# Spreading operand preparation over half rounds, freeing a conversion buffer earlier, and respacing normalisation steps in a fused attention and expert kernel

## The chip, the cores and the metric

The kernel runs on one core of a Trainium2 chip. The metric is the device time of one execution in microseconds (us): the kernel before takes 2182.73 us, the median of three runs (2181.15 to 2185.93).

A core has five engines with a queue each, and each works its queue strictly in order: TensorE (PE: matrix products, with its weight loads listed apart as PEld), VectorE (DVE), ScalarE (ACT), GpSimd (POOL) and SyncE (SP), which here issues the DMA transfers. An instruction that waits holds everything behind it on its engine. Matrix products land in PSUM banks; all else lies in SBUF.

## The reference

```python
# attention: q, k, v of 4 x 8 heads x 576 x 64, causal by blocks of 64
x = attention(q, k, v)                      # 2304 tokens x 512
h = x @ w_in                                # 512 -> 2048
x = np.maximum(0.01 * h, h) @ w_out         # 2048 -> 512
P = exp(x @ w_gate - max)                   # 2304 x 8 experts
for _ in range(8):                          # the normalisation
    P /= P.sum(1) + 1e-9; P /= P.sum(0) + 1e-9; P *= 2304 / 8
out = sum over e of P[:, e:e+1] * (np.maximum(x @ w1[e], 0) @ w2[e])   # 512 -> 1024 -> 512
```

The first three parts feed one another. w_in and w_out arrive as 64-bit numbers; all else is float32.

## The kernel before

**Split operands.** TensorE multiplies a 32-bit format (fp32r) with fewer mantissa bits than float32. So each operand is split into a high part (a cast on ACT) and a low part (value minus high part, a subtraction on DVE), and a product is three: high by high, high by low, low by high. `w_split` does this for weights, `x_step` for x, `halves` for sums of weights. Tile names end in h and l accordingly (w1h, w1l, xhS, xlS).

**Stages.** After attention (to about 260 us) comes the first MLP: its 2048 hidden columns are taken in two halves (e = 0, 1), each in 8 chunks (f) of 128, and the tokens in five blocks of 512, 512, 512, 384 and 384. For each (e, block, f) `hidden` makes 128 hidden columns (L514) and `second` multiplies them by w_out into four PSUM banks o0 to o3 (L543), two chunks behind. At f = 7 the four banks are emptied into xa, for e = 0 by copies on ACT and DVE (L552, L554); the next block's first `second` needs those banks.

**Conversion.** The 64-bit weights are rebuilt from their words by `bits_steps`: six operations on DVE (begin L156, bound L160, shift L166, sign L172, power L178, rest L184), then for the second half of the weights an addition on POOL (`store`, L208) and a DMA to a scratch tensor in DRAM (s_in, s_out), from which half e = 1 loads its weights. Raw words lie in two buffers (wraw), intermediate words in two of wa and one of wb: wb is taken at shift and given back when POOL has read it. The list `bits` holds loads and steps of 16 such units; the main loop takes six entries from it after each chunk, from block 1 on (L857 to L860).

**The experts.** The second MLP runs in three passes of 768 tokens (p). Each pass has 8 experts of 4 column groups, taken two at a time: a round is 14 products of six matmuls (`product`, L733, the "half round") and then six combinations of twelve (`combine`, L787), 16 rounds in a pass, 48 in all. The products use fast-matrix-multiplication terms of x: A11, A12, A22 and sums S1 to S4, made by `x_step` (a subtraction on POOL, L717, in place in xa; the cast on ACT, L719; the low part on DVE, L720). A pass's last round must make the next pass's seven operands: this is called the turn here; there are two (pass 0 to 1 near 1170 us, 1 to 2 near 1672 us). In the turn `behind(...)` puts two operands behind each of the first three combinations and one behind the fourth, together with the round's usual work: the next groups' weights (`w1_sums` on POOL L679 to L682, `w1_s`, `w1_a` on ACT and DVE L695, L696, `w2_split` L131, L132) and the emptying of the output banks (L795 to L800).

**The normalisation** runs beside the first rounds: `gate_chunk` for six late token tiles, `gate_max`, `gate_exp`, then eight times `rows`, a small matmul for the column sums (L636) and `columns`; sums stand at fixed products and combinations.

**Order.** A scheduler puts each engine's queue in order from the order of the code and its own time estimates; `in_order` chains PE's products, and `behind` places steps after the latest relu instructions (`last_taken`).

Of the kernel before, what the change touches and what calls it, by code (L numbers as in the profile page):

```python
# [8 lines left out]
F32 = mybir.dt.float32  # L9
# [3 lines left out]
ALU = mybir.AluOpType  # L13
AX = mybir.AxisListType
# [22 lines left out]
def block_attention_mlp_moe(  # L37
# [15 lines left out]
    nc = tc.nc  # L53
# [92 lines left out]
    def bits_steps(which, f):  # L146
# [35 lines left out]
        def rest():  # L182
            bf = st["bf"] = st["b"].bitcast(F32)
            nc.vector.scalar_tensor_tensor(  # L184
                out=bf, in0=st["low"], scalar=2.0 ** -52, in1=bf, op0=ALU.mult, op1=ALU.mult
            )
# [316 lines left out]
    hid, o_ps = {}, {}  # L503
# [30 lines left out]
    def second(e, b, f):  # L534
# [3 lines left out]
        for s in range(KC):  # L538
# [7 lines left out]
            if f == FC - 1:  # L546
                at = t0
                while at < t0 + n:
                    p, to = at // TP, min(t0 + n, (at // TP + 1) * TP)
                    a, o = xv[p][:, s, at - p * TP:to - p * TP], o_ps[s][:, at - t0:to - t0]  # L550
                    if e == 0 and (p > t0 // TP if t0 // TP < (t0 + n - 1) // TP else s % 2):
                        nc.vector.tensor_copy(out=a, in_=o)  # L552
# [71 lines left out]
    def rows():  # L624
# [7 lines left out]
        nc.vector.tensor_reduce(out=st["cs"], in_=pr.rearrange("p t e -> p e t"), axis=AX.X, op=ALU.add)  # L632
# [78 lines left out]
    def x_step(p, k):  # L711
# [4 lines left out]
        if change:  # L716
            nc.gpsimd.tensor_tensor(out=src, in0=change[0], in1=change[1], op=ALU.subtract)  # L717
# [109 lines left out]
    for m, (e, b, f) in enumerate(todo):  # L827
# [23 lines left out]
        if e == 0 and b == 0:  # L851
            if f < len(late):
                bits_load(*late[f])
            if 0 < f <= len(late):
                for step in bits_steps(*late[f - 1]):
                    step()
        elif e == 0 and bits:  # L857
            for _ in range(6):
                if bits:
                    bits.pop(0)()  # L860
# [42 lines left out]
    norm = [gate_max, gate_exp, rows]  # L903
# [11 lines left out]
    order = [*range(TC // 2, TC), *range(TC // 2)]  # L915
    for n in range(0, NGR, 2):
        p, e, i = groups[n]
        turn = e == E - 1 and i + 2 == NI and p + 1 < NPASS
        for m, (g, k, name, begins, f, *a) in enumerate(first_products):
            product(n + g, k, name, begins)  # L920
            f(n + g, *a)
            if n == 0 and m in (1, 3, 5):
                in_order(gate_chunk)(NPASS - 1, TC // 2 + m // 2, o_bank())
            if n == 0 and m == 2:
                w2_split(1)
                w2_load(2)
                w2_load(3)
            if n and norm and m in (1, 4):
                normal(o_bank)
            if m == 5:  # L930
                w1_sums(n + 2)
                if not n:
                    norm.pop(0)()
        if owed and not norm:
# [6 lines left out]
            lambda: w2_split(n + 3),  # L941
            lambda: (w2_load(n + 4), w2_load(n + 5)),
        ]
        for m, t in enumerate(order):
            combine(n, t)
            if turn:
                behind(*(lambda k=k: x_step(p + 1, k) for k in terms[2 * m:2 * m + 2]))
            behind(more[m])
            if norm and m in ((0, 2, 5) if n == 0 else (2, 5)):
                normal(h_bank)  # L950
# [33 lines left out]
```

## Time and profile before

| | before |
|---|---|
| device time, median of 3 (lowest to highest) | 2182.73 us (2181.15 to 2185.93) |
| the profiled execution's own time | 2183.18 us |
| its span, first to last instruction | 2181.4 us |
| mean granted TensorE clock | 0.995 |
| busy PE / DVE / ACT / POOL | 2141.8 / 1473.5 / 917.2 / 510.2 us |

Busy shares say which engine is nearly always at work: PE, 98% of the span. Whatever shortens this kernel must therefore take work from PE or one of the stretches in which PE waits. The list of waits names these by the line that waited and the line that released it; "idle before" in a row of the timeline is the same wait at its place. Times in a timeline run from the span's start; a duration of one matmul is longer than the distance to the next, since matmuls overlap, so losses are read from start to start.

### The profile page before, as it was taken

What the parts mean: (1) busy time and instruction counts of PE and PEld (TensorE: products, weight loads), DVE (VectorE), ACT (ScalarE), POOL (GpSimd) and SP (SyncE); (2) the same over time, 40 slices, a digit from 0 to 9 for tenths busy, and PEclk for the clock granted to TensorE, in tenths of its full rate; (3) what the DMA queues carried; (4) which work ended last, traced back from release to release, by engine and by line L of the source; (5) the groups of instructions that cost most, each with busy time, mean ns of one, the idle gap of its engine ahead of it and who ended that gap; (6) DMA issues with size and microseconds to landing.
All of it is one profiled execution on the core that took longest, in us unless ns stands there. A gap on an engine that the chain in (4) does not pass through costs nothing.

```text
span 2181.4 us, 29500 instructions
## 1 busy us (share of the span) xinstructions
PE 2141.8 (98%) x10932; PEld 1904.3 (87%) x10932; DVE 1473.5 (68%) x2467; ACT 917.2 (42%) x1916; POOL 510.2 (23%) x549
## 2 busy tenths in 40 slices
PE   7999999999999999999999999999999999999999
PEld 6787787998899899899988989998898899989998
DVE  7999777343356866766677677666767766676665
ACT  6776522232334434443344344434443443344332
POOL 3334332000022122221223222222223221222220
PEclk9999999999999999999999999999999999999999
DMA  4333134020002122211222222122213212221120
GB/s 103 84 88 85 41 112 144 25 68 1 1 21 77 39 78 78 78 50 67 78 78 68 78 78 67 50 78 78 73 44 106 78 49 68 78 78 56 61 78 29
DMA packets 157248, 146.63 MB, mean 67 GB/s; under 512 B 62640, under 2 KB 126128, under 8 KB 157104
## 3 DMA queue, kind: packets, MB, share of 16 engines
q1 hardware_dynamic: 157104, 144.75, 22.1%
q8 instruction: 86, 1.41, 0.3%
q14 instruction: 58, 0.48, 0.1%
HBM read 135.81 MB, written 8.91 MB: 66 GB/s over the span
## 4 chain that ended last, share of the span: by engine, by line
PE 79%; DVE 3%; issue 0%; ACT 0%; POOL 0%; ACTq 0%; DVEq 0%
PE o L787 34%; PE h_ps L733 32%; PE o L543 7%; PE h_ps L514 6%; DVE w1l L696 1%; DVE xlS L720 0%; DVE w2l L132 0%; DVE xa L800 0%; PE l_ps L597 0%; DVE xa L795 0%; DVE xlA L720 0%; DVE c L750 0%; ACT w1h L695 0%; POOL xa L717 0%; PE o L586 0%
## 5 line engine op out<-in xcount | busy, mean ns | idle before, releaser
L787 PE MATMUL o<-w2h,xhlate 128*128 128x512 f32 x1152 | 402.4, 390 | 0.0
L787 PE MATMUL o<-w2h,xllate 128*128 128x512 f32 x1152 | 401.6, 389 | 0.0
L679 POOL TENSOR_TENSOR wa<-wraw 128x256 f32<-128x256 f32 x96 | 87.6, 912 | 1271.3 <-DVE w1l L696 1174.9
L741 ACT COPY s<-h_ps 128x384 f32<-128x384 f32 x288 | 138.5, 481 | 565.1 <-PE h_ps L733 565.1
L750 DVE TENSOR_TENSOR c<-h_ps,s 128x384 f32<-128x384 f32 x288 | 155.7, 555 | 324.8 <-PE h_ps L733 314.8
L733 PE MATMUL h_ps<-xhS,w1h 128*128 128x384 f32 x768 | 258.1, 336 | 0.0
L733 PE MATMUL h_ps<-xlS,w1h 128*128 128x384 f32 x768 | 257.4, 335 | 0.0
L733 PE MATMUL h_ps<-xhS,w1l 128*128 128x384 f32 x768 | 257.2, 335 | 0.0
L787 PEld LDWEIGHTS o<-w2h,xllate 128*128 128x128 f32 x1152 | 216.3, 188 | 45.4
L787 PEld LDWEIGHTS o<-w2h,xhlate 128*128 128x128 f32 x1152 | 216.2, 188 | 43.4
L800 DVE SCALAR_TENSOR_TENSOR xa<-o,pr,xa 128x512 f32<-128x512 f32 x264 | 189.6, 741 | 52.5 <-PE o L787 52.4
L787 PE MATMUL o<-w2l,xhlate 128*128 128x512 f32 x576 | 224.7, 390 | 0.0
L787 PE MATMUL o<-w2l,xllate 128*128 128x512 f32 x576 | 224.4, 390 | 0.0
L733 PE MATMUL h_ps<-xhA,w1l 128*128 128x384 f32 x576 | 194.1, 337 | 10.3 <-DVE w1l L696 10.3
L733 PE MATMUL h_ps<-xhA,w1h 128*128 128x384 f32 x576 | 193.6, 336 | 0.0
L733 PE MATMUL h_ps<-xlA,w1h 128*128 128x384 f32 x576 | 193.2, 335 | 0.0
L696 DVE TENSOR_TENSOR w1l<-wraw,w1h 128x512 fp32r<-128x512 f32 x192 | 175.8, 954 | 0.1
L696 DVE TENSOR_TENSOR w1l<-wa,w1h 128x512 fp32r<-128x512 f32 x192 | 166.8, 871 | 0.0
L756 ACT ACTIVATE xllate<-c 128x384 fp32r<-128x384 f32 x144 | 75.7, 525 | 185.0 <-DVE c L750 185.0
L132 DVE TENSOR_TENSOR w2l<-wraw,w2h 128x1024 fp32r<-128x1024 f32 x100 | 147.2, 1473 | 1.1 <-ACT w2h L131 1.1
L733 PEld LDWEIGHTS h_ps<-xhS,w1h 128*128 128x128 f32 x768 | 145.0, 189 | 0.0
L733 PEld LDWEIGHTS h_ps<-xlS,w1h 128*128 128x128 f32 x768 | 144.9, 189 | 0.0
(164 smaller groups left out, 4321.8 us busy)
## 6 DMA issues: line engine op xcount, KB each, us to landing
wraw<-in_moe_w_dram SPq DMA_DIRECT2D x192, 512.0 KB, 4.2
wraw<-in_moe_w_in_dram SPq DMA_DIRECT2D x16, 512.0 KB, 3.8
wraw<-in_moe_w_out_dram SPq DMA_DIRECT2D x16, 512.0 KB, 3.6
out_dram<-xa SPq DMA_DIRECT2D x18, 256.0 KB, 2.3
qraw<-in_q_dram SPq DMA_DIRECT2D x32, 128.0 KB, 2.4
kraw<-in_k_dram SPq DMA_DIRECT2D x32, 128.0 KB, 2.6
vz<-in_v_dram SPq DMA_DIRECT2D x32, 128.0 KB, 2.3
s_in<-wa SPq DMA_DIRECT2D x8, 256.0 KB, 3.1
```

The lines of the kernel that those rows point to most:

```text
L132: nc.vector.tensor_tensor(out=lo, in0=raw, in1=f32(hi), op=ALU.subtract)
L514: nc.tensor.matmul(ps[:, 0:n], w[:, c, cols], x, start=c == 0 and s == 0, stop=c == KC - 1 and s == 2,)
L543: nc.tensor.matmul(o_ps[s][:, 0:n], w[:, cut], h[:, 0:n], start=f == 0 and m == 0, stop=f == FC - 1 and m == 2)
L679: nc.gpsimd.tensor_tensor(out=one[:, 0], in0=a21, in1=a22, op=ALU.add)
L696: nc.vector.tensor_tensor(out=lo, in0=x, in1=f32(hi), op=ALU.subtract)
L733: mm = nc.tensor.matmul(ps, w[:, c], x[:, c], start=first and c == 0 and s == 0, stop=c == 1 and s == 2, skip_group_check=True,)
L741: nc.scalar.copy(out=t, in_=bank[n, name][:, 0:HT])
L750: nc.vector.tensor_tensor(out=c, in0=x, in1=part[n, add], op=ALU.add)
L756: nc.scalar.activation(out=hi, in_=x, func=AF.Relu),
L787: mm = nc.tensor.matmul(o, h, w, start=m == 0, stop=m == 11)
L800: nc.vector.scalar_tensor_tensor(out=a, in0=o, scalar=pr[:, tt, e:e + 1], in1=a, op0=ALU.mult, op1=ALU.add)
```

## The change

Four edits: the conversion's last DVE step writes into the raw buffer instead of wb for units of the second half; the conversion steps of e = 0 are taken only after chunks 1 to 6 of a block and stand behind the latest DVE copy of a block end; the normalisation's sums stand at other products and combinations; and the next pass's operands are made in three places (A11 and the subtractions of S1 and S3 at product 2 of the turn's round; S1, S2, S3 in its combinations; S4, A12, A22 from product 3 of the round after), with the subtractions on DVE rather than POOL for the passes after the first. One w2 split and one w2 load of the turn move to product 2 of the round after. The number of rounds, products and matmuls is the same.

```diff
         def rest():
-            bf = st["bf"] = st["b"].bitcast(F32)
+            bf = st["bf"] = (st["b"] if f < FC else st["low"]).bitcast(F32)
             nc.vector.scalar_tensor_tensor(
-                out=bf, in0=st["low"], scalar=2.0 ** -52, in1=bf, op0=ALU.mult, op1=ALU.mult
+                out=bf, in0=st["low"], scalar=2.0 ** -52, in1=st["b"].bitcast(F32), op0=ALU.mult, op1=ALU.mult
             )
...
-                        nc.vector.tensor_copy(out=a, in_=o)
+                        taken[:] = [nc.vector.tensor_copy(out=a, in_=o)]
...
-        nc.vector.tensor_reduce(out=st["cs"], in_=pr.rearrange("p t e -> p e t"), axis=AX.X, op=ALU.add)
+        t = nc.vector.tensor_reduce(out=st["cs"], in_=pr.rearrange("p t e -> p e t"), axis=AX.X, op=ALU.add)
+        last_taken.append(getattr(t, "ins", t))
...
-    def x_step(p, k):
+    def x_src(p, k, make):
...
-        if change:
-            nc.gpsimd.tensor_tensor(out=src, in0=change[0], in1=change[1], op=ALU.subtract)
+        if make and change:
+            eng = nc.vector if p else nc.gpsimd
+            eng.tensor_tensor(out=src, in0=change[0], in1=change[1], op=ALU.subtract)
+        return src
+
+    def x_step(p, k, make=True):
+        src = x_src(p, k, make)
...
-        elif e == 0 and bits:
-            for _ in range(6):
-                if bits:
-                    bits.pop(0)()
+        elif e == 0 and 0 < f < FC - 1:
+            with tc.issue_after(getattr(taken[0], "ins", taken[0])):
+                for _ in range(6):
+                    if bits:
+                        bits.pop(0)()
...
-            if n == 0 and m in (1, 3, 5):
-                in_order(gate_chunk)(NPASS - 1, TC // 2 + m // 2, o_bank())
-            if n == 0 and m == 2:
-                w2_split(1)
-                w2_load(2)
-                w2_load(3)
-            if n and norm and m in (1, 4):
+            if n == 0 and 0 < m <= TC // 2:
+                in_order(gate_chunk)(NPASS - 1, TC // 2 + m - 1, o_bank())
+            if (n == 0 or turned) and m == 2:
+                w2_split(n + 1)
+                if n == 0:
+                    w2_load(2)
+                w2_load(n + 3)
+            if turned and 2 < m < 6:
+                x_step(p, terms[m + 1])
+            if n == 0 and m == TC // 2:
+                gate_max()
+            if norm and m in ((1, 5) if n else (5,)):
                 normal(o_bank)
+            if turn and m == 2:
+                x_step(p + 1, "A11")
+                for k in ("S1", "S3"):
+                    x_src(p + 1, k, True)
...
-            lambda: w2_split(n + 3),
-            lambda: (w2_load(n + 4), w2_load(n + 5)),
+            lambda: None if turn else w2_split(n + 3),
+            lambda: (w2_load(n + 4), None if turn else w2_load(n + 5)),
         ]
         for m, t in enumerate(order):
             combine(n, t)
-            if turn:
-                behind(*(lambda k=k: x_step(p + 1, k) for k in terms[2 * m:2 * m + 2]))
+            if norm and m in (1, 4):
+                normal(h_bank)
             behind(more[m])
-            if norm and m in ((0, 2, 5) if n == 0 else (2, 5)):
-                normal(h_bank)
+            if turn and m < 3:
+                behind(lambda: x_step(p + 1, terms[m + 1], m == 1))
+        turned = turn
```

Line numbers of the changed kernel are one to six higher: L697 there is L696 here, L719 the subtraction, L725 and L726 the cast and low part of `x_step`, L806 is L800.

**Place 1: the end of block 1 of e = 0, DVE.** Before, in DVE's queue (wa, wb and wraw are the conversion's buffers, g and hl the hidden chunk, o0 to o3 the banks that are emptied):

```order
L160 TENSOR_SCALAR wa_4055<-wa_4055 128x512
L166 TENSOR_SCALAR wb_4058<-wa_4055 128x512
L522 TENSOR_TENSOR g_3694<-h_ps_3679,g_3694 128x512
L172 SCALAR_TENSOR_TENSOR wa_4055<-wraw_3973,wb_4058 128x512
L552 COPY xa1_2981<-o0_3407 128x256
L552 COPY xa1_2981<-o1_3411 128x256
L178 TENSOR_SCALAR wb_4058<-wa_4055 128x512
L156 TENSOR_SCALAR wa_4103<-wraw_4017 128x512
L524 TENSOR_TENSOR hl_3693<-g_3694,hh_3692 128x512
L552 COPY xa1_2981<-o2_3415 128x256
L184 SCALAR_TENSOR_TENSOR wb_4058<-wraw_3973,wb_4058 128x512
L552 COPY xa1_2981<-o3_3419 128x256
```

In the changed kernel at the same block end:

```order
L522 TENSOR_TENSOR g_3644<-h_ps_3629,g_3644 128x512
L524 TENSOR_TENSOR hl_3643<-g_3644,hh_3642 128x512
L522 TENSOR_TENSOR g_3685<-h_ps_3670,g_3685 128x512
L552 COPY xa1_2981<-o0_3407 128x256
L552 COPY xa1_2981<-o1_3411 128x256
L524 TENSOR_TENSOR hl_3684<-g_3685,hh_3683 128x512
L552 COPY xa1_2981<-o2_3415 128x256
L552 COPY xa1_2981<-o3_3419 128x256
L166 TENSOR_SCALAR wb_3778<-wa_3667 128x512
L156 TENSOR_SCALAR wa_3819<-wraw_3665 128x512
L172 SCALAR_TENSOR_TENSOR wa_3667<-wraw_3621,wb_3778 128x512
L160 TENSOR_SCALAR wa_3819<-wa_3819 128x512
```

Before, six conversion steps stand among these rows, ahead of the four copies and between them; now the copies stand behind hidden chunks alone, and the conversion goes on after the last. L184 now writes wraw.

**Place 2: the first turn, DVE and ACT.** Before, DVE's queue after the first output bank of the turn's combinations (xl is a low part of x, w1l and w2l those of weights, xa0 the output of the pass that ends, xa1 the x of the next):

```order
L720 TENSOR_TENSOR xlA11_10440<-xa1_2981,xhA11_10439 128x768
L696 TENSOR_TENSOR w1l_10449<-wa_10340,w1h_10448 128x512
L696 TENSOR_TENSOR w1l_10449<-wa_10341,w1h_10448 128x512
L696 TENSOR_TENSOR w1l_10455<-wraw_10204,w1h_10454 128x512
L696 TENSOR_TENSOR w1l_10455<-wraw_10204,w1h_10454 128x256
L800 SCALAR_TENSOR_TENSOR xa0_2980<-o2_10460,pr_2987,xa0_2980 128x512
L720 TENSOR_TENSOR xlS4_10509<-xa1_2981,xhS4_10508 128x768
L720 TENSOR_TENSOR xlA12_10513<-xa1_2981,xhA12_10512 128x768
L132 TENSOR_TENSOR w2l_10551<-wraw_10284,w2h_10550 128x1024
L800 SCALAR_TENSOR_TENSOR xa0_2980<-o3_10493,pr_2987,xa0_2980 128x512
L132 TENSOR_TENSOR w2l_10570<-wraw_10286,w2h_10569 128x1024
L720 TENSOR_TENSOR xlS1_10445<-xa1_2981,xhS1_10444 128x768
```

In the changed kernel, from the first output bank on:

```order
L697 TENSOR_TENSOR w1l_10446<-wa_10346,w1h_10445 128x512
L697 TENSOR_TENSOR w1l_10446<-wa_10347,w1h_10445 128x512
L697 TENSOR_TENSOR w1l_10452<-wraw_10204,w1h_10451 128x512
L806 SCALAR_TENSOR_TENSOR xa0_2980<-o2_10461,pr_2987,xa0_2980 128x512
L697 TENSOR_TENSOR w1l_10452<-wraw_10204,w1h_10451 128x256
L726 TENSOR_TENSOR xlS1_10458<-xa1_2981,xhS1_10457 128x768
L726 TENSOR_TENSOR xlS3_10517<-xa1_2981,xhS3_10516 128x768
L806 SCALAR_TENSOR_TENSOR xa0_2980<-o3_10489,pr_2987,xa0_2980 128x512
L132 TENSOR_TENSOR w2l_10538<-wraw_10284,w2h_10537 128x1024
L719 TENSOR_TENSOR xa1_2981<-xa1_2981 128x2x384
L697 TENSOR_TENSOR w1l_10505<-wa_10476,w1h_10504 128x512
```

The low parts of S4 and A12 have moved ahead of these rows (between the last relu steps of the round), that of A11 into the round's products, and one of two w2 splits too; S1 and S3 have moved from behind the w2 splits to ahead of the remaining one. The two casts that end this stretch on ACT, and what follows them, before:

```order
L695 CAST w1h_10516<-wa_10486 128x512
L719 CAST xhS2_10476<-xa1_2981 128x768
L719 CAST xhA22_10544<-xa1_2981 128x768
L741 COPY s1_10599<-h_ps_10592 128x384
L741 COPY s1_10608<-h_ps_10601 128x384
L741 COPY s5_10617<-h_ps_10610 128x384
```

and in the changed kernel:

```order
L696 CAST w1h_10504<-wa_10477 128x512
L725 CAST xhS2_10485<-xa1_2981 128x768
L725 CAST xhA22_10640<-xa1_2981 128x768
L747 COPY s1_10580<-h_ps_10573 128x384
L747 COPY s1_10589<-h_ps_10582 128x384
L747 COPY s5_10598<-h_ps_10591 128x384
```

They stand in the same places: the next round's first copies out of PSUM (s1, L741, now L747) remain behind the casts of S2 and A22.

**Place 3: the end of e = 0, DVE.** Before, ending with the first low part of e = 1's first chunk, hl_4613 (the w1l and w2l are weights of e = 1, loaded from the scratch tensors):

```order
L132 TENSOR_TENSOR w1l_4632<-wraw_4595,w1h_4631 128x1024
L522 TENSOR_TENSOR g_4502<-h_ps_4487,g_4502 128x384
L132 TENSOR_TENSOR w2l_4560<-wraw_4521,w2h_4559 128x1024
L524 TENSOR_TENSOR hl_4501<-g_4502,hh_4500 128x384
L522 TENSOR_TENSOR g_4538<-h_ps_4523,g_4538 128x384
L524 TENSOR_TENSOR hl_4537<-g_4538,hh_4536 128x384
L132 TENSOR_TENSOR w1l_4716<-wraw_4675,w1h_4715 128x1024
L522 TENSOR_TENSOR g_4578<-h_ps_4563,g_4578 128x384
L132 TENSOR_TENSOR w2l_4636<-wraw_4597,w2h_4635 128x1024
L524 TENSOR_TENSOR hl_4577<-g_4578,hh_4576 128x384
L522 TENSOR_TENSOR g_4614<-h_ps_4599,g_4614 128x512
L524 TENSOR_TENSOR hl_4613<-g_4614,hh_4612 128x512
```

In the changed kernel, up to the row before the same low part:

```order
L178 TENSOR_SCALAR wb_4516<-wa_4513 128x512
L184 SCALAR_TENSOR_TENSOR wraw_4425<-wraw_4425,wb_4516 128x512
L132 TENSOR_TENSOR w1l_4553<-wraw_4507,w1h_4552 128x1024
L522 TENSOR_TENSOR g_4535<-h_ps_4520,g_4535 128x384
L524 TENSOR_TENSOR hl_4534<-g_4535,hh_4533 128x384
L132 TENSOR_TENSOR w2l_4557<-wraw_4509,w2h_4556 128x1024
L522 TENSOR_TENSOR g_4578<-h_ps_4563,g_4578 128x384
L132 TENSOR_TENSOR w1l_4632<-wraw_4595,w1h_4631 128x1024
L524 TENSOR_TENSOR hl_4577<-g_4578,hh_4576 128x384
L132 TENSOR_TENSOR w2l_4636<-wraw_4597,w2h_4635 128x1024
L522 TENSOR_TENSOR g_4614<-h_ps_4599,g_4614 128x512
L132 TENSOR_TENSOR w1l_4716<-wraw_4675,w1h_4715 128x1024
```

The last conversion step (wraw_4425), which stood two blocks ahead, now stands among these chunks. The four weights between w1l_4553 and w1l_4716 follow it closely, and w1l_4716, two chunks ahead of hl_4613 before, stands directly in front of it.

## Rows read from the trace of the kernel before

**Rows 1.** Windows: length, busy PE, PEld, DVE, ACT, POOL with instructions, PE clock, DMA.

```profile
357.50:364.30 6.80, 5.85 (x14) 4.60 (x15) 6.50 (x13) 2.38 (x5) 1.28 (x1) 0.50 0.43 146
1176.70:1183.50 6.80, 3.78 (x12) 3.78 (x13) 6.80 (x8) 2.64 (x5) 5.68 (x6) 0.50 0.43 150
1200.00:1640.00 440.00, 440.00 (x2215) 399.00 (x2214) 300.33 (x428) 179.66 (x341) 103.08 (x116) 1.00 0.23 70
```

**Rows 2.** Waits of PE: what waited, releaser: us in all, times, longest.

```profile
PE h_ps L733 <- DVE w1l L696: 10.3, 2, 5.2
...
PE o L543 <- DVE xa L552: 4.3, 2, 3.1
...
PE h_ps L636 <- DVE cs L632: 0.8, 1, 0.8
...
PE o L636 <- ACT s L741: 0.6, 1, 0.6
PE o L636 <- DVE cs L632: 0.5, 1, 0.5
```

**Rows 3.** Chain that ended last, two rounds: start, us, what.

```profile
1194.91 16.36 PE o L787 x72
1211.27 14.58 PE h_ps L733 x84
```

**Rows 4.** Timeline, PE, end of block 1: start us, us, instruction, idle before it.

```profile
354.93 0.39 PE L514 MATMUL h_ps<-xhfirst,w1l 128*128 128x512 f32 x1
358.45 0.79 PE L543 MATMUL o<-hh,w2h 128*128 128x512 f32 x1 [3.13 <-DVE xa L552]
...
364.47 0.39 PE L543 MATMUL o<-hh,w2l 128*128 128x512 f32 x1
```

**Rows 5.** Timeline, PE, first turn.

```profile
1174.23 0.34 PE L733 MATMUL h_ps<-xlA,w1h 128*128 128x384 f32 x1
1179.72 0.69 PE L733 MATMUL h_ps<-xhA,w1l 128*128 128x384 f32 x1 [5.15 <-DVE w1l L696]
...
1183.64 0.34 PE L733 MATMUL h_ps<-xhS,w1l 128*128 128x384 f32 x1
```

**Rows 6.** Timeline, DVE, end of block 1.

```profile
356.43 0.43 DVE L166 TENSOR_SCALAR wb<-wa 128x512 uint32<-128x512 uint32 x1 [1.15 <-POOL wa L208]
...
357.38 0.68 DVE L172 SCALAR_TENSOR_TENSOR wa<-wraw,wb 128x512 uint32<-128x512 uint32 x1
357.98 0.75 DVE L552 COPY xa<-o 128x256 f32<-128x256 f32 x2
```

**Rows 7.** Timeline, DVE, combinations of an undisturbed round.

```profile
1196.99 0.56 DVE L757 SCALAR_TENSOR_TENSOR xllate<-c,xllate 128x384 fp32r<-128x384 f32 x1 [0.65 <-ACT xllate L756]
...
1201.57 1.76 DVE L132 TENSOR_TENSOR w2l<-wraw,w2h 128x1024 fp32r<-128x1024 f32 x1
...
1203.91 1.21 DVE L132 TENSOR_TENSOR w2l<-wraw,w2h 128x1024 fp32r<-128x1024 f32 x1
...
1205.64 1.56 DVE L696 TENSOR_TENSOR w1l<-wraw,w1h 128x512 fp32r<-128x512 f32 x2
1207.12 1.22 DVE L696 TENSOR_TENSOR w1l<-wa,w1h 128x512 fp32r<-128x512 f32 x1
```

**Rows 8.** Timeline, DVE, first turn.

```profile
1160.26 0.95 DVE L720 TENSOR_TENSOR xlA<-xa,xhA 128x768 fp32r<-128x768 f32 x1
...
1166.68 1.93 DVE L720 TENSOR_TENSOR xlS<-xa,xhS 128x768 fp32r<-128x768 f32 x1
```

**Rows 9.** Timeline, DVE, products of a round before the first turn.

```profile
1149.62 0.56 DVE L750 TENSOR_TENSOR c<-h_ps,s 128x384 f32<-128x384 f32 x1 [6.62 <-PE h_ps L733]
```

**Rows 10.** Timeline, ACT, first turn.

```profile
1179.15 0.83 ACT L719 CAST xhA<-xa 128x768 fp32r<-128x768 f32 x1 [1.38 <-POOL xa L717]
1179.89 0.47 ACT L741 COPY s<-h_ps 128x384 f32<-128x384 f32 x1
```

**Rows 11.** Timeline, POOL, first turn.

```profile
1165.77 2.02 POOL L717 TENSOR_TENSOR xa<-xa 128x768 f32<-128x768 f32 x1
1167.75 1.46 POOL L680 TENSOR_TENSOR wa<-wa,wraw 128x256 f32<-128x256 f32 x1
```

**Rows 12.** DMA issues: count, KB each, median us to landing.

```profile
wraw<-s_in SPq DMA_DIRECT2D x4, 512.0 KB, 4.3
```

**Rows 13.** Groups by line: count, busy us, mean ns, idle before.

```profile
L208 POOL TENSOR_TENSOR wa<-wa,wb 128x512 f32<-128x512 f32 x16 | 21.4, 1336 | 69.9 <-DVE wb L184 66.5 <-issue 3.5
```

**Rows 14.** Timeline, ACT, combinations of an undisturbed round.

```profile
1198.72 2.00 ACT L131 CAST w2h<-wraw 128x1024 fp32r<-128x1024 f32 x2
```

More of the change, by code (lines that the diff above doesn't have):

```diff
@@ L501, in block_attention_mlp_moe @@
     nc.gpsimd.tensor_tensor(out=gparts[:, :, 1, :], in0=gate, in1=f32(gparts[:, :, 0, :]), op=ALU.subtract)
-    hid, o_ps = {}, {}
+    hid, o_ps, taken = {}, {}, []
     def hidden(e, b, f):
@@ L901, in block_attention_mlp_moe @@
     ]
-    norm = [gate_max, gate_exp, rows]
+    norm = [gate_exp, rows]
     for n in range(SINKHORN):
@@ L915, in block_attention_mlp_moe @@
     order = [*range(TC // 2, TC), *range(TC // 2)]
+    turned = False
     for n in range(0, NGR, 2):
@@ L921, in block_attention_mlp_moe @@
             f(n + g, *a)
-            if n == 0 and m in (1, 3, 5):
-                in_order(gate_chunk)(NPASS - 1, TC // 2 + m // 2, o_bank())
-            if n == 0 and m == 2:
-                w2_split(1)
-                w2_load(2)
-                w2_load(3)
-            if n and norm and m in (1, 4):
+            if n == 0 and 0 < m <= TC // 2:
[10 more added lines that the diff above has]
+            if norm and m in ((1, 5) if n else (5,)):
                 normal(o_bank)
+            if turn and m == 2:
+                x_step(p + 1, "A11")
+                for k in ("S1", "S3"):
+                    x_src(p + 1, k, True)
             if m == 5:
                 w1_sums(n + 2)
-                if not n:
-                    norm.pop(0)()
         if owed and not norm:
```

## The prediction

> **What bounds the kernel now.** I read four views in this order. The windows first: over 440 us of the experts' rounds PE is busy for 440.00 us at clock 1.00 while DVE works 300 and POOL 103 [rows 1]. The reader should see that nothing but PE counts there, and that the change, which leaves every matmul in place, can gain nothing in such a stretch. Then the list of PE's waits: behind the start, the large ones at lines that the change touches are the two of 10.3 us together on w1l (the two turns), two of 4.3 us on the copies that empty the output banks (block ends, the longer 3.1 us), and three of the normalisation, 0.8 + 0.6 + 0.5 = 1.9 us [rows 2]. Third, the windows again: after the long waits PE runs at a granted clock of 0.50, which is 1.2 GHz instead of 2.4 GHz, in 357.5 to 364.3 and in 1176.7 to 1183.5 [rows 1]. So a wait costs more than its idle time, and a loss must be read from start to start. Last the chain, for the undisturbed distances: 72 matmuls of a combination phase take 16.36 us, 0.227 us each, and 84 of a product phase 14.58 us, 0.174 us each [rows 3].
>
> With these the losses are:
> - End of block 1: from the last matmul before the wait at 354.93 to the first at full pace at 364.47 there are 15 intervals [rows 4]. They took 9.54 us and are worth 15 x 0.227 = 3.41: loss 6.1.
> - The other block end: 4.3 - 3.1 = 1.2 us of wait [rows 2]; I take 1.2.
> - First turn: 13 intervals from 1174.23 to 1183.64 [rows 5] took 9.41 and are worth 2.26: loss 7.15. The second turn waits as long (10.3 is twice 5.2), so I take the same: 14.3.
> - Normalisation: 1.9.
>
> Together 23.5 us of 2183.18.
>
> **Block ends.** The cause shows in DVE's queue: at 356.43 a shift step (L166) has waited 1.15 us for POOL to give wb back, then come the hidden chunk, a sign step of 0.68 and only at 357.98 the copies that PE wants [rows 6]. In the changed order the conversion stands behind all four copies (place 1), and wb is released by DVE itself. A copy then waits for its bank and for at most one hidden chunk of 0.7 us. I count both losses as gone: 1.2 + 6.1 = 7.3. If a wait survived it would be one conversion step, 0.68 us; bounds 6.6 to 7.3. What the conversion pays is below.
>
> **Turns.** The w1l that PE waits for is the A11 of the second group, wanted by the third matmul of the second product. If C is the start of the combinations, that is C + 16.36 + 8 x 0.174 = C + 17.75. In an undisturbed round C is 1194.91 [rows 3] and this w1l is the first half of the pair at 1205.64 [rows 7], so done near 1206.5, C + 11.6: six microseconds early. The old turn puts x's low parts, slowed, and the wait for POOL's sums in front of it.
>
> In the changed order (place 2) I add to the undisturbed C + 11.6:
> - S1's and S3's low parts, 2 x 0.95 (the undisturbed one is at 1160.26 [rows 8]): + 1.9
> - the subtraction for S2 on DVE. No row shows a subtraction of x on DVE; the nearest is the low part, also a 128x768 float32 subtraction out of two SBUF operands, 0.95; bounds 0.95 and the 1.93 that this form took beside POOL. I take 0.95.
> - S4's and A12's low parts between the round's last relu steps, 1.9, of which DVE's idle time there hides the 0.65 [rows 7] and a few tenths: + 1.1
> - one w2l fewer, 1.21 [rows 7]: - 1.2
>
> This gives C + 14.4, or C + 15.4 with the dear subtraction; the 3.3 us in hand are the cover. A11 and the two other subtractions and the displaced w2l are in the products of the turn, where DVE waits 6.62 us in one piece [rows 9]; 3 x 0.95 + 1.2 = 4.1 fit. The displaced casts fit on ACT, busy 41% of the rounds [rows 1].
>
> What is late next is the end of the chain: behind A11 come the rest of that pair (0.8), another w1l of 1.22 [rows 7], an output bank of 0.7, the subtraction for A22 (0.95) and S2's low part (0.95), to C + 18.9 or 19.0. S2 is the fourth product and reads its low part at C + 16.36 + 19 x 0.174 = C + 19.66. On ACT the cast of A22 waits for its subtraction (C + 18.0), takes 0.83, and the copy of the first product out of PSUM stands behind it (place 2), 0.47 more [rows 10]: C + 19.3, wanted at C + 19.48 by that same product, which adds into the bank. Two tenths are within the error of this addition. I take a wait of 0.4 per turn, cost 0.8; bounds 0 and 3.9 of wait each. The upper bound lets four steps of this chain be slowed as the low part of S at 1166.68 was, 1.93 against 0.95 [rows 8]: 4 x 0.98 = 3.9.
>
> Is that slowing likely? At 1165.77 POOL's subtraction began, 2.02 us long [rows 11]; the low part that was queued at 1166.68 ended 0.8 us after it ended, just its undisturbed length. So it stood still, and did not run slowly. The Trainium skill, "SBUF — State Buffer", section "Who interferes with whom", says that a DVE instruction with two SBUF inputs and a GpSimd instruction that reads SBUF share one port pair and that the second to start is blocked for the whole of the first. The trace agrees with that. It cuts both ways here: POOL's subtractions go, but its sums for the next weights remain, and the new DVE subtractions are now subject to them. By the rule each blocked step adds what is left of a sum; if two of the four sums hit, A11 is still in time and the end of the chain is some 1 us late. The undisturbed round has these sums in it already, which is why I stay at 0.4.
>
> **Normalisation.** The first of the three waits should go, since the sums before it move a combination earlier. In the second round the weight splits are now held behind the column reduction: 1.56 + 1.22 + 0.7 of w1l and a w2l stand ahead of the next column step, which the sum at the second product of the third round waits for. I take it that one wait of 1.3 replaces the three: gain 0.6; bounds 1.9 (all gone) and -2 (the wait at half clock).
>
> **The conversion, now later.** Conversions that were done in block 2 now run into block 4, and share two raw buffers with the eight weight loads of e = 1 (place 3). From the end of block 3 I count three units and eight weights through two buffers. A unit: load 4.3 at most [rows 12], six DVE steps of 0.43 to 0.68 [rows 6], POOL's addition 1.34 [rows 13], some 8.5. A weight: load 4.3, cast 1.0 [rows 14], low part 1.21, some 6.5. Sum 3 x 8.5 + 7 x 6.5 = 71 up to the last w1l, 35.5 through two buffers. Behind that w1l in DVE's queue stands the first hidden chunk of e = 1 (hl_4613). It is wanted after block 4: 8 chunks of 24 matmuls of 384 columns, 192 x 0.174 = 33.4 us, and the hidden chunks of 512 columns issued before its end, about 4: 37.5. So 2 us in hand. POOL now reads low words two apart; no row shows that; between 1.34 and twice that, which would use 3 x 1.34 / 2 = 2.0 of them. I take 0.3 of wait; bounds 0 and 4.
>
> **Sum.** 7.3 + 14.3 - 0.8 + 0.6 - 0.3 = 21.1 us. 2183.18 - 21.1 = 2162.1 us. The profiled execution lies 0.45 above the median of the runs, within their spread; I forecast by it.
>
> **The rivals.**
> - *The turns stay late by another wait.* The ACT queue (the copy behind the cast of A22) or blocked DVE steps hold PE 3 us or more, and the clock halves again: the wait of 3.1 us at block 1 lost 6.1 [rows 2, 4]. Each turn then gives back 1 of 7.15. For: the chain ends within 0.2 us of its need, and ACT's order is unchanged. Against: 3.3 us in hand at A11, and the slow POOL subtractions gone. Time: 2162.1 + 2 x 5.7 = 2173.5. A single turn so, or half the wait, gives 2168.
> - *Slower: raw buffers refill one after another.* SP's queue holds a store that waits for POOL and behind it the loads that would fill the free buffer. If the two never overlap, the 71 us above stand against 37.5, and the start of e = 1 is 33 us late: 2162 + 33 = 2195. It decides where less than a third of the refills overlap: the 71 us are then over 59, and the lateness passes the gain of 21. Against: loads stand between stores in both orders, and DVE, which does the steps, is busy only about two thirds.
> - *The change only moves waits.* The four edits fix nothing on the path: the copies wait for a conversion again, the turns for something else. Time 2183. Against: the order shows both causes gone.
>
> **Chances.** The forecast, with its small terms off by a few us (2158 to 2168): 0.70. The turns late: 0.19. Waits only moved: 0.06. Raw buffers: 0.05, of which a little ends between. Range 2158 to 2174, which leaves about 0.14 out, most of it above. A difference of 0.2%, 4.4 us, is about what runs of this kernel can tell from none. Faster by more than that 0.89, within it 0.06, slower 0.05.
>
> **What would show it.** In the list of waits the lines of w1l on L739 (10.3) and xa on the block ends (4.3) are gone or under 1 us; the clock is 1.00 in windows round 360, 1180 and 1682, mean above 0.998; no row L166 waits for POOL's L208. Right behind the turns a wait of PE on ACT s or on DVE xlS of 0 to 1 us. A wait at the sum L637 of about 1.3 us near 740. Conversion steps until about 445, and no wait over 1 us at the start of e = 1. Wrong it would be if the half clock is still seen after a turn, or if PE waits for w1l or hl between 465 and 480.

## The result and the profile after

The changed kernel takes 2159.70 us (median of four runs, 2159.07 to 2159.82), the kernel before, in the same comparison, 2184.33 us (2181.15 to 2186.26): a ratio of 0.9888, 95% interval 0.9871 to 0.9905. The forecast was 2162.1 us, between 2158 and 2174. The two profiled executions stand at 2183.18 and 2159.59 us, 23.6 us apart; the forecast had 21.1.

PE is now busy for 2135.3 us of a span of 2157.8 us, 99%, at a mean granted clock of 0.998. Its waits after attention, by line and releaser (us in all, times, longest), answer to [rows 2]:

```profile
PE h_ps L514 <- DVE g L522: 0.7, 1, 0.7
...
PE o L637 <- DVE cs L632: 0.4, 1, 0.4
```

The reader should see what is no longer there: w1l on the products (10.3 us), xa on the emptied banks (4.3 us) and two of the three column sums. The windows at the end of block 1, at the start of e = 1 and at both turns (length; busy PE, PEld, DVE, ACT, POOL, with instructions; PE clock; DMA share, GB/s) answer to [rows 1]:

```profile
345.00:355.00 10.00, 10.00 (x46) 8.29 (x45) 7.34 (x15) 3.74 (x8) 1.31 (x1) 1.00 0.00 0
460.00:467.00 7.00, 7.00 (x31) 5.38 (x30) 5.79 (x8) 4.38 (x7) 0.98 (x2) 1.00 0.43 150
1163.00:1170.00 7.00, 7.00 (x41) 6.92 (x40) 4.10 (x6) 3.18 (x7) 4.62 (x4) 1.00 0.53 187
1665.00:1672.00 7.00, 7.00 (x42) 6.92 (x41) 4.56 (x9) 2.82 (x6) 0.00 (x0) 1.00 0.00 1
```

PE is busy without a break and at clock 1.00 in all four. The chain of work at the first turn (start, us, what) shows the same from start to start:

```profile
1147.24 16.36 PE o L793 x72
1163.60 14.58 PE h_ps L739 x84
```

These are the 16.36 and 14.58 us of an undisturbed round [rows 3]: the turn now costs nothing.

DVE at the end of block 1 (start, us, instruction, idle before it), against [rows 6]:

```profile
347.38 0.69 DVE L522 TENSOR_TENSOR g<-h_ps,g 128x512 f32<-128x512 f32 x1 [3.37 <-ACT g L521]
347.99 0.95 DVE L552 COPY xa<-o 128x256 f32<-128x256 f32 x2
349.04 0.69 DVE L524 TENSOR_TENSOR hl<-g,hh 128x512 fp32r<-128x512 f32 x1
349.64 0.75 DVE L552 COPY xa<-o 128x256 f32<-128x256 f32 x2
350.31 0.42 DVE L166 TENSOR_SCALAR wb<-wa 128x512 uint32<-128x512 uint32 x1
```

Between the copies stands one low part of a hidden chunk, and the conversion's shift comes after the fourth. At the first turn, the end of the chain, DVE, then ACT, then POOL:

```profile
1160.90 1.02 DVE L697 TENSOR_TENSOR w1l<-wraw,w1h 128x512 fp32r<-128x512 f32 x2
...
1163.10 0.95 DVE L719 TENSOR_TENSOR xa<-xa 128x768 f32<-128x768 f32 x1
1163.97 0.95 DVE L726 TENSOR_TENSOR xlS<-xa,xhS 128x768 fp32r<-128x768 f32 x1
```

```profile
1164.08 0.83 ACT L725 CAST xhA<-xa 128x768 fp32r<-128x768 f32 x1 [2.83 <-DVE xa L719]
1164.82 0.47 ACT L747 COPY s<-h_ps 128x384 f32<-128x384 f32 x1
```

```profile
1154.41 0.73 POOL L681 TENSOR_TENSOR wa<-wa,wraw 128x256 f32<-128x256 f32 x1
...
1161.12 2.01 POOL L680 TENSOR_TENSOR wa<-wraw 128x256 f32<-128x256 f32 x1 [5.09 <-DVE w1l L697]
1163.20 2.32 POOL L681 TENSOR_TENSOR wa<-wa,wraw 128x256 f32<-128x256 f32 x1
```

With C = 1147.24 the A11 weights (the first of the pair at 1160.90, which alone takes 0.69) are ready at 1161.6, C + 14.35, where they are wanted at C + 17.75; S2's low part is ready at 1164.9, C + 17.7 (wanted at 19.66), and the first copy out of PSUM at 1165.3, C + 18.05 (wanted at 19.48).

### The profile page after: what moved, and what is told of

The parts are those of the page before. It is cut to its first block, busy times and chain, and to the rows that moved or that the text cites. A ratio compares the mean times of both kernels' runs of the same rounds, so it can differ in the third digit from the quotient of the medians.

```text
span 2157.8 us, 29493 instructions
## 1 busy us (share of the span) xinstructions
PE 2135.3 (99%) x10932; PEld 1900.2 (88%) x10932; DVE 1473.6 (68%) x2475; ACT 917.7 (43%) x1916; POOL 496.9 (23%) x541
## 4 chain that ended last, share of the span: by engine, by line
PE 93%; DVE 5%; ACT 1%; issue 0%; POOL 0%; ACTq 0%; DVEq 0%; POOLq 0%
PE o L793 36%; PE h_ps L739 32%; PE h_ps L514 9%; PE o L543 9%; PE av L373 3%; PE sc L322 2%; PE tr L349 1%; DVE nmax L323 1%; DVE ex L342 1%; ACT ex L328 0%; DVE w1l L697 0%; DVE kTl L281 0%; DVE qbdl L274 0%; DVE rsum L338 0%; DVE wb L184 0%
## 5 line engine op out<-in xcount | busy, mean ns | idle before, releaser
L747 ACT COPY s<-h_ps 128x384 f32<-128x384 f32 x288 | 138.5, 481 | 539.7 <-PE h_ps L739 539.5
L806 DVE SCALAR_TENSOR_TENSOR xa<-o,pr,xa 128x512 f32<-128x512 f32 x264 | 189.4, 741 | 52.1 <-PE o L793 52.1
L697 DVE TENSOR_TENSOR w1l<-wraw,w1h 128x512 fp32r<-128x512 f32 x192 | 172.4, 936 | 0.1
L697 DVE TENSOR_TENSOR w1l<-wa,w1h 128x512 fp32r<-128x512 f32 x192 | 160.1, 836 | 0.0
```

The lines of the kernel that those rows point to most:

```text
L697: nc.vector.tensor_tensor(out=lo, in0=x, in1=f32(hi), op=ALU.subtract)
L747: nc.scalar.copy(out=t, in_=bank[n, name][:, 0:HT])
L806: nc.vector.scalar_tensor_tensor(out=a, in0=o, scalar=pr[:, tt, e:e + 1], in1=a, op0=ALU.mult, op1=ALU.add)
```

## The experiments

"From start to start" is the time that a stretch of PE's matmuls took beyond the undisturbed 0.227 and 0.174 us each, added up over a disturbance, as in the forecast. One thing has to be known to read the totals: in two of the profiles below PE's first instruction starts at 9.8 us instead of 6.3, which is not due to any edit (last section), and attention, which no edit touches, ended between 254.7 and 257.7 us in the others. So a difference of one or two us is read from the stage, and not from the median.

**Conversion edits alone.** The kernel before with

```diff
+            bf = st["bf"] = (st["b"] if f < FC else st["low"]).bitcast(F32)
...
+        elif e == 0 and 0 < f < FC - 1:
+            with tc.issue_after(getattr(taken[0], "ins", taken[0])):
```

> The kernel before with the two edits of the conversion alone (L184 into the raw buffer, conversion steps off the block ends). Theory (the gain is the sum of separate stalls with their half-clock stretches): the losses of 1.5 and 6.1 us at the two block ends go, 0.3 us comes at the start of e = 1, 2183.2 - 7.4 = 2175.8 us; both turns still wait 5.2 us at half clock. Rival (the edits need each other, the conversion at a later time also slows what follows): a smaller gain, 2179 or more, or PE waits at the start of e = 1.

Measured: 2175.28 us (2174.33 to 2178.94), ratio 0.9966 (0.9955 to 0.9978). No wait on L552 is left, both turns still wait 5.2 us and lose 7.3 and 7.0 us from start to start. At the start of e = 1 there is a loss of 0.9 instead of the 0.3 expected. The theory holds, and this part gives 7.8 us by the medians.

**The new turn alone.** The kernel before with the edits of `x_step`, of the round's products and combinations, and of the w2 split and load, without the others.

> The kernel before with the new turn alone (operands in three places, subtractions on DVE, one w2 split and load later). Theory: the two losses of 7.2 and 6.9 us go, 2183.2 - 14.1 = 2169.1 us; the wait of 3.1 us at block 1 stays, with its half clock. Rival (part of the turns' gain is due to POOL's queue being free of the conversion or to the normalisation's new places): less than 12 us.

Measured: 2168.42 us (2166.01 to 2169.21), ratio 0.9931 (0.9919 to 0.9944): 14.7 us. No w1l, xlS or s is waited for at the turns. The conversion, whose code is the one of before, is not disturbed in quite the same way: its waits are 5.2 us instead of 4.3, and the block ends lose 9.0 us from start to start instead of 7.6.

```profile
PE o L543 <- DVE xa L552: 5.2, 2, 3.3
```

So from the first L514 to the end this profile is 12.7 us shorter than the one of before: the 14.1 of the turns, less 1.4 lost at the block ends. The 14.7 between the medians has some 2 us that this stage does not show.

**The normalisation alone.** The kernel before with the edits of `rows`, `norm` and the places of the sums.

> The kernel before with the normalisation's new places alone. Theory: three waits of 1.9 us (2.9 us from start to start) become one of 0.4 (0.9 from start to start), 2183.2 - 2.0 = 2181.2 us. My forecast had 0.6 us for it. Rival: nothing that can be measured, as some 2 us of either sign are lost in the spread; then the list of waits decides.

Measured: 2182.58 us against 2183.11, ratio 0.9998 (0.9989 to 1.0007): nothing that the runs can tell. In the profile the three waits have become one:

```profile
PE h_ps L734 <- DVE w1l L697: 10.3, 2, 5.1
...
PE o L543 <- DVE xa L552: 4.6, 2, 2.7
...
PE o L637 <- DVE cs L632: 0.4, 1, 0.4
```

From start to start the sums lose 0.9 us instead of 2.9, as expected. Of what the edit does not touch, the turns lost 15.0 instead of 14.1 in this execution and the block ends 6.7 instead of 7.6, which cancel; from the first L514 to the end it is 1.75 us shorter. In the times the gain is not shown: the interval reaches from 2.4 us less to 1.5 more. The three parts by their medians are 7.8 + 14.7 + 0.5 = 23.0 us, and the whole change 24.6 (23.6 between the profiles): within these spreads the parts add up.

**Which of the two conversion edits?** First only L184 into the raw buffer:

```diff
+            bf = st["bf"] = (st["b"] if f < FC else st["low"]).bitcast(F32)
```

> The kernel before with the first conversion edit alone: L184 writes the raw buffer, so that wb comes free by DVE itself, the steps stay at the block ends. Theory (the block ends lose because conversion steps stand in front of the copies in DVE's queue, and the wait for POOL's wb is only the larger part): no L166 waits for L208 any more, block 1's wait falls from 3.1 to 1 to 2 us without the half clock, 2183.2 - 5 = 2178 us (2176 to 2181). Rival A (wb's wait is all of it): 2175.8 as with both edits. Rival B (the place in the queue is all of it): 2183.

Measured: 2185.97 us (2184.88 to 2187.14), ratio 1.0012 (1.0003 to 1.0021): slower by some 3 us, outside all three expectations. The list of waits has L552 three times, 7.6 us, and the block ends lose 10.6 us from start to start instead of 7.6. DVE at the end of block 1, then PE behind it:

```profile
357.63 1.50 DVE L156 TENSOR_SCALAR wa<-wraw 128x512 uint32<-128x512 uint32 x1
359.16 0.43 DVE L160 TENSOR_SCALAR wa<-wa 128x512 f32<-128x512 f32 x1
359.62 0.43 DVE L166 TENSOR_SCALAR wb<-wa 128x512 uint32<-128x512 uint32 x1
360.08 0.69 DVE L172 SCALAR_TENSOR_TENSOR wa<-wraw,wb 128x512 uint32<-128x512 uint32 x1
360.81 0.43 DVE L178 TENSOR_SCALAR wb<-wa 128x512 uint32<-128x512 uint32 x1
361.15 0.69 DVE L522 TENSOR_TENSOR g<-h_ps,g 128x512 f32<-128x512 f32 x1
361.75 0.68 DVE L184 SCALAR_TENSOR_TENSOR wraw<-wraw,wb 128x512 f32<-128x512 uint32 x1
362.35 0.75 DVE L552 COPY xa<-o 128x256 f32<-128x256 f32 x2
```

```profile
362.83 0.79 PE L543 MATMUL o<-hh,w2h 128*128 128x512 f32 x1 [4.72 <-DVE xa L552]
```

No step waits for POOL's L208 any more, but a unit's six steps now follow one another closely and a whole unit, 357.63 to 362.43, stands in front of the copies. Its first step takes 1.50 us, where L156 took 0.43 at the same block end before: POOL's addition of the unit ahead (L208, 357.04 to 358.84) runs beside it. That is 1.1 of the 1.6 us by which the longest wait grew (4.72 against 3.13); the closer steps are left as the cause of the rest, which no run separates. The wait of 1.15 us that [rows 6] show is not what holds the copies. Then only the place:

```diff
+            with tc.issue_after(getattr(taken[0], "ins", taken[0])):
+                for _ in range(6):
```

> The kernel before with the second conversion edit alone: the steps stand behind the copies of a block end and are taken after chunks 1 to 6, wb is still given back by POOL. In the run with only the other edit the block ends got worse (7.6 us of waits instead of 4.3). Theory A (the place in DVE's queue is the cause): both block-end losses of together 7.6 us go; each unit of the conversion now also waits some 1.2 us for POOL, so the chain of the last units and the weights of e = 1 is 3 to 4 us later than with both edits, where nothing was in hand, and PE waits some 3 us at the start of e = 1, with a half clock perhaps: 2183 - 7.6 + 3 to 6 = 2178.5 to 2181.5. Theory B (wb's wait is the cause and both edits are needed for it): waits of 2 us or more on L552 remain.

Measured: 2179.42 us (2174.27 to 2182.03), ratio 0.9968 (0.9957 to 0.9979). Theory A is right on the block ends: L552 is gone from the waits. It is wrong on the start of e = 1, where PE lost nothing, although DVE waited again for POOL:

```profile
DVE wb L166 <- POOL wa L208: 7.9, 9, 1.2
```

The 4 us more than with both edits come from before the part that was edited: the first L514 stands at 261.33 us instead of 255.60, 3.6 us of it by a late start of this profiled execution. Seven of the ten runs lie between 2179.2 and 2182.1 and three between 2174.2 and 2177.0; that the seven all started late is likely, but the others have no trace:

```profile
9.82 1.09 PE L286 MATMUL qm<-ident,qraw 128*128 128x128 f32 x4 [9.82 <-DVE ident L458]
```

From the first L514 to the end it takes 1916.5 us, and the kernel with both edits 1918.0. So the place is all of the gain at the block ends; the first edit gave nothing there.

**Subtractions on POOL again.** The changed kernel with

```diff
-            eng = nc.vector if p else nc.gpsimd
+            eng = nc.gpsimd
```

> The changed kernel with the eight subtractions of x of the two turns on POOL again. Theory (the gain of the turns comes from the earlier place; the chain to the A11 weights had 3.3 us in hand): DVE has 1.9 us less to do in the combinations, POOL's two subtractions there take 2.0 to 2.3 us each behind its sums, PE waits under 1 us per turn, 2159.6 to 2161.5. Rival (one engine blocks the other for the whole of an instruction, and the engine was the point of the change): DVE's low parts stand still for 4 us and more in the combinations, each turn waits 2 us or more: 2164 to 2172.

Measured: 2161.81 us from four runs in two groups, 2158.98 and 2159.56, 2164.07 and 2164.49; the profiled one is of the upper and has the late start. The turns lose 0.4 us each. POOL, DVE and PE at the first turn:

```profile
1160.62 5.28 POOL L719 TENSOR_TENSOR xa<-xa 128x768 f32<-128x768 f32 x2 [0.89 <-DVE xlS L726]
```

```profile
1162.00 2.21 DVE L132 TENSOR_TENSOR w2l<-wraw,w2h 128x1024 fp32r<-128x1024 f32 x1
1164.12 2.33 DVE L697 TENSOR_TENSOR w1l<-wa,w1h 128x512 fp32r<-128x512 f32 x1
```

```profile
1170.77 0.44 PE L739 MATMUL h_ps<-xlS,w1h 128*128 128x384 f32 x1 [0.16 <-DVE xlS L726]
```

While POOL's two subtractions ran (5.28 us), a w1l that takes 0.68 us elsewhere took 2.33; PE waits 0.16 us at the place where the chain ends. The engine of the subtractions was worth under a microsecond; the places were worth the 14.

**Everything back in the combinations.** The changed kernel with A11 and the subtractions of S1 and S3 moved:

```diff
-            if turn and m == 2:
-                x_step(p + 1, "A11")
...
+            if turn and m == 0:
+                behind(lambda: x_step(p + 1, "A11"), lambda: [x_src(p + 1, k, True) for k in ("S1", "S3")])
```

> The changed kernel with A11's split and the subtractions of S1 and S3 in the turn's combinations instead of its products, on DVE as there: 2.9 us more in front of the chain. In the changed kernel's trace the weights of A11 were ready 3.2 us before their use, and the copy of the first product 1.5 us before. Theory (these are the true reserves): the A11 weights are still in time, S2's parts and the copy behind A22's cast come 3 us late, with half clock: 2159.6 + 2 x 3 to 6 = 2166 to 2172, PE waiting on s or xlS and not on w1l. Rival (DVE takes it up in its idle time): 2159 to 2161.

Measured: 2173.03 us (2171.94 to 2176.31), ratio 0.9946 (0.993 to 0.9962). PE and ACT at the first turn:

```profile
1167.70 0.44 PE L739 MATMUL h_ps<-xhS,w1h 128*128 128x384 f32 x1 [2.01 <-ACT xhS L725]
1169.89 0.69 PE L739 MATMUL h_ps<-xlS,w1h 128*128 128x384 f32 x1 [1.75 <-DVE xlS L726]
```

```profile
1166.82 0.83 ACT L725 CAST xhS<-xa 128x768 fp32r<-128x768 f32 x1 [2.64 <-DVE xa L719]
1167.55 0.85 ACT L747 COPY s<-h_ps 128x384 f32<-128x384 f32 x2
```

PE waits for S2's cast, 2.01 us, and then for its low part, 1.75, and not for w1l: the place that the forecast named as next. The clock was 0.50 from 1168.5 to 1169.8, within the second wait, and from 1171 to 1175 us. Each turn loses 6.7 us from start to start, which is the whole of the 13.3 between the medians. The A11 weights still have time, as their reserve says.

**What a wait costs.** The changed kernel with reductions on DVE in seven rounds, ahead of the weights:

```diff
+            for _ in range(times):
+                t = nc.vector.tensor_reduce(out=st["gmax"], in_=xa[2][:, 0:wide], axis=AX.X, op=ALU.max)
...
-            lambda: (w1_s(n + 3), w1_a(n + 3)),
+            lambda: late_w1(n),
```

> The changed kernel with idle work on DVE (8 to 14 maximum reductions of x of the last pass, results unused until overwritten) in seven rounds of the second pass, so that the A11 weights come late by estimates of 0.3, 0.9, 1.2, 2.4, 3.0, 4.2 and 5.4 us. What does a wait cost from start to start? Theory: the half clock follows waits from some length between 1.2 and 3.1 us (the kernel before: 1.2 us lost 1.5, 3.1 lost 6.1, 5.2 lost 7), and costs 1.7 to 3.4 us beside the idle time, however long the wait. Rival (the cost grows with the wait): 5.4 us loses twice as much beside its idle time as 2.4.

Measured in one execution (2197.64 us; the waits came out otherwise than estimated, from 1.2 to 6.1 us; four of the seven, PE; then the windows behind the second, the third, the fifth and the seventh: length, busy PE with matmuls, PE clock, DMA share, GB/s):

```profile
1229.38 0.44 PE L739 MATMUL h_ps<-xhA,w1l 128*128 128x384 f32 x1 [1.21 <-DVE w1l L697]
```

```profile
1295.41 0.69 PE L739 MATMUL h_ps<-xhA,w1l 128*128 128x384 f32 x1 [3.85 <-DVE w1l L697]
```

```profile
1497.02 0.44 PE L739 MATMUL h_ps<-xhA,w1l 128*128 128x384 f32 x1 [3.18 <-DVE w1l L697]
```

```profile
1633.63 0.69 PE L739 MATMUL h_ps<-xhA,w1l 128*128 128x384 f32 x1 [6.05 <-DVE w1l L697]
```

```profile
1295.50:1302.50 7.00, 7.00 (x26) 0.60 0.22 75
1365.00:1372.00 7.00, 7.00 (x29) 0.69 0.23 76
1497.00:1504.00 7.00, 6.98 (x40) 1.00 0.22 75
1634.00:1641.00 7.00, 7.00 (x28) 0.64 0.24 75
```

| wait, us | 1.21 | 2.46 | 3.18 | 3.85 | 4.62 | 4.78 | 6.05 |
|---|---|---|---|---|---|---|---|
| lost from start to start, us | 1.5 | 2.7 | 3.5 | 6.7 | 6.5 | 7.1 | 8.8 |

The three waits up to 3.18 us cost themselves and 0.3 us. At the four from 3.85 us on the clock fell to its lower level, 1.2 GHz, and this cost 1.8 to 2.9 us more, not more for the longest wait than for the shortest: the theory against the rival. But the theory's length is not there, and no limit can be read from this run alone. At block ends of other kernels shorter waits than 3.18 us were followed by the half clock: 3.13 us before [rows 4], 2.71 with the normalisation alone, and 1.96 with the new turn alone (clock 0.50 from 312.4 to 315.7 us, 3.8 lost from start to start), while 1.86 with the normalisation alone was not. In the run above it came after a wait of 2.01 us, within the second one.

**Without the first conversion edit.** The changed kernel with L184 writing wb again:

> The changed kernel without its first conversion edit: wb is given back by POOL again, the raw buffer by DVE. With the place alone the profile showed no loss at the block ends and none at the start of e = 1, where kernels with both edits lose 0.3 to 1.5 us. Theory (the edit adds nothing, and holds the raw buffers, through which the next loads must go, until POOL has added): the loss at the start of e = 1 goes, 2159.0 us; DVE waits some 8 us for POOL's L208 again, which costs nothing. Rival (the edit is needed for the conversion to end in time once the turns are new): PE waits 2 us or more at 460 to 470, 2162 us and more. A start of PE that is 3.6 us later, seen in some profiles at the first instructions, would add to any of these.

Measured: 2158.31 us (2157.8 to 2159.29); the changed kernel in the same comparison, below, 2158.80. The loss at 460 to 470 us is gone from the profile (it was 0.3), DVE waits 7.9 us for L208. As the theory has it, but the difference of 0.5 us is not one that the runs can tell.

**The run before with the sums one product later too:**

```diff
-            if norm and m in ((1, 5) if n else (5,)):
+            if norm and m in ((2, 5) if n else (5,)):
```

> As the run before, and the normalisation's sums at products 2 and 5 of the later rounds instead of 1 and 5: the column sum that PE waited 0.4 us for (0.9 us from start to start) has one product, 1.0 us, more time. Theory: no wait of the second MLP's stages is left on the lines of the change, 2158.2 us. Rival (the sum at product 5 then waits): 2159 or more.

Measured: 2158.78 us (2157.71 to 2158.91). The list of waits has nothing left behind attention but the 0.7 of L514, as above; the sums' L637 is gone from it. From start to start PE loses 2.1 us after 255 us, and 3.1 in the changed kernel beside it. In the time no gain can be seen: neither of these two can be called faster than the changed kernel.

**A raw buffer that comes free later.**

```diff
         def store():
             a = st["af"]
+            nc.gpsimd.tensor_copy(out=st["b"].bitcast(F32), in_=st["bf"])
```

> The changed kernel with one more POOL instruction in each unit's store (a copy of the low words back into wb, 1.3 us, unused), so that a raw buffer comes free 1.3 us later. What does the forecast's slower rival cost, and how near was it? Theory (two buffers, three units after the end of block 3, nothing in hand): the last w1l and with it the first hidden chunk of e = 1 come 2 to 4 us later, PE waits as long there: 2161.5 to 2166. Rival (the refills overlap, there is reserve): under 2161.

Measured: 2159.72 us (2157.22 to 2160.85). The theory falls: PE lost nothing at the start of e = 1. (The copy took 0.85 us at the median, not 1.3.) DVE shows why:

```profile
454.43 1.23 DVE L132 TENSOR_TENSOR w1l<-wraw,w1h 128x1024 fp32r<-128x1024 f32 x1 [1.47 <-ACT w1h L131]
455.57 0.69 DVE L525 TENSOR_TENSOR hl<-g,hh 128x512 fp32r<-128x512 f32 x1
456.94 1.23 DVE L132 TENSOR_TENSOR w2l<-wraw,w2h 128x1024 fp32r<-128x1024 f32 x1 [0.68 <-ACT w2h L131]
...
460.14 1.23 DVE L132 TENSOR_TENSOR w1l<-wraw,w1h 128x1024 fp32r<-128x1024 f32 x1 [0.45 <-ACT w1h L131]
```

The first hidden chunk of e = 1 (hl at 455.57) now stands in front of the last three weight splits, where the changed kernel has it behind the last w1l:

```profile
461.35 1.23 DVE L132 TENSOR_TENSOR w1l<-wraw,w1h 128x1024 fp32r<-128x1024 f32 x1 [0.85 <-ACT w1h L131]
462.50 0.68 DVE L524 TENSOR_TENSOR hl<-g,hh 128x512 fp32r<-128x512 f32 x1
```

The scheduler, which knew of the slower store, had turned their order round. The chain that the forecast added up is no chain of the data; it holds for one order only, and what the slower rival would really cost was not reached. The time is the one of the rival expectation; its reason, a reserve in the old order, was not tested.

**The changed kernel once more,** as the measure of these three:

> The changed kernel itself, on the same chip as the three others: 2159.6 us where PE starts at 6.3 us, 2163.2 us where it starts at 9.8. It shows whether the late start is met with the changed kernel too.

Measured: 2158.80 us (2157.91 to 2160.38); PE started at 6.26 us in its profile, and no run was near 2163.

## Why the prediction was right, point by point

- **What bounds the kernel, and the losses** (23.5 us from waits and half clocks): right. The profiles are 23.6 us apart, and the losses from start to start after attention fell from 26.2 to 3.0 us.
- **Block ends**, 7.3 us: right in size. The term for the shorter wait was mis-sized, 1.2 us where 1.5 was lost from start to start. Of the two causes named only one is a cause. "And wb is released by DVE itself" stands in the forecast as a second reason; alone it made the kernel 3 us slower, and the place alone, with the waits for POOL still there, gave the whole gain.
- **Turns**, 14.3 - 0.8: the mechanism, the reserve and the next late step were right, the remaining wait was not there. The A11 weights were forecast at C + 14.4 and came at C + 14.35; that it is so near is in part luck, since single terms were off (S1's and S3's low parts together took 2.37 us at 1155.35, not 1.9). The end of the chain was mis-sized by 1.2 us: S2's low part came at C + 17.7 instead of 18.9, the copy at C + 18.05 instead of 19.3. I had taken the rest of the weights at the 1.22 and 0.8 us of an undisturbed round [rows 7], where POOL's sums stand in their way. Here DVE was first and POOL stood still: its sums took 2.01 and 2.32 us, where one takes 0.73 undisturbed. The Trainium skill, "SBUF — State Buffer", section "Who interferes with whom", says that whichever of the two starts first holds the shared ports and the other one is blocked; these rows agree. Each sum stood until the run of DVE subtractions beside it was over (1162.5 and 1164.9), not only the first of them. So the forecast's sentence on blocked steps had the loser the wrong way round at the end of the chain; at 1155.35, where a sum had begun at 1155.23, DVE was the loser, as it says.
- **Normalisation**, 0.6: mis-sized; start to start 2.0 us came back. One wait replaced three, as said, but of 0.43 us and not 1.3: the column reduction was ready at 731.7 us, 19.6 after the round's combinations began near 712.1 (its products began at 697.30 and took 14.58, with two sums of 0.12 between them), and I had it most of a microsecond later.
- **Start of e = 1**, 0.3: right in the changed kernel (0.27 us from start to start, 0.33 in the repetition), but by luck. The other profiles with both conversion edits and this order, whose further edits do not touch this stage, lost 0.8 to 1.5 us there, and the reserve of 2 us belonged to one order of the queue: a slower store lost nothing. The doubling that was feared for POOL's addition of words two apart did not come: it took 1.39 us on average, 1.34 before.
- Together: 0.8 not paid at the turns, 1.4 more at the normalisation and 0.3 at the first block end, less 0.2 because the second turn had lost 6.9 and not 7.15, are 2.3 of the 2.5 us by which the forecast was too high.
- **The rivals.** The turns' other wait was the nearest: 1.4 us of reserve kept it out, and 2.9 us more on DVE brought it. That its 2173.0 is nearly the forecast's 2173.5 is luck: a turn lost 6.7 us and not the 6.1 assumed, from a base 2.4 us lower. Waits that only move were not seen. For the slower rival nothing was found, and no run reached its condition.

## What to carry to other kernels

A wait in front of a late copy names the last thing it waited for; what to look for is everything that stands ahead of the copy in its engine's queue, and moving that is worth more than making it faster (here the faster release alone cost 3 us). Where a periodic task overloads one phase, add the new steps to an undisturbed period's row and find the step that is late next: here the answer was good to 1.2 us. Read waits from start to start: where the half clock followed one, it cost 1.8 to 2.9 us beside the wait in the run with seven of them. Between 1.9 and 3.2 us both happened, so look at the granted clock and do not go by the length.

## What the runs showed of the hardware

In two of the profiles DVE's first five small instructions took 7.70 us instead of 4.12, and PE, which waits for the identity matrix that they begin, started at 9.82 us instead of 6.25. From the profile with the place alone (start, us, instruction):

```profile
0.88 7.70 DVE L453 TENSOR_SCALAR ramp<-ramp 128x1 f32<-128x1 f32 x5
8.61 0.21 DVE L455 STREAM_TRANSPOSE ramp_t<-ramp 128x32 f32<-128x32 f32 x1
```

Nothing ahead of these rows differs between the kernels; why some executions have it stays open. It is as large as most effects here, and would be 3.6 of the 5.0 us between the two groups in the runs with the subtractions on POOL (2159 and 2164), of which only one run has a trace. The other surprise is that waits of 2.46 and 3.18 us left the clock at 1.00 and ones of 1.96 and 3.13 us did not.
